# Attention of a transformer block: written orders for two steps' score and maxima tiles, by the kind of step

## The chip, the cores and the metric

The kernel is one transformer block in float32. It runs as one program on one core of a Trainium2 chip. The metric is the device time of the whole program in microseconds (us). Before the change it is 2805.59 us, the median of three runs (2802.46 to 2810.95). A profile was taken of one execution. The engines are named as the profile names them: PE (TensorE, with PEld for its weight loads), DVE (VectorE), ACT (ScalarE), POOL (GpSimd) and SP (the queue that issues most DMAs).

## What is computed

```python
def _A_ref(x, wqkv, wo):                       # S = 2048 rows, D = 576, H = 32 heads of Dh = 18
    qkv = (x @ wqkv).reshape(B, S, 3, H, Dh).transpose(2, 0, 3, 1, 4)
    q, k, v = qkv[0], qkv[1], qkv[2]
    scores = jnp.einsum("bhqd,bhkd->bhqk", q, k) * Dh ** -0.5
    p = _softmax(scores, axis=-1)
    o = jnp.einsum("bhqk,bhkd->bhqd", p, v)
    return o.transpose(0, 2, 1, 3).reshape(B, S, D) @ wo

mod = (_silu(c) @ w_mod).reshape(1, 6, 1, -1)  # sa, ca, ga, sb, cb, gb
h = _layernorm(x) * (1 + ca) + sa
x = x + ga * _A_ref(h, wqkv, wo)
h = _layernorm(x) * (1 + cb) + sb
x = x + gb * ((_sigmoid(h @ w_gate) * (h @ w_up)) @ w_down)
```

The change touches the scores, the softmax and their product with v, nothing else.

## The kernel before

The program has three parts: projections of q, k and v up to about 235 us, attention from there to about 1533 us, and the gated layer to the end. Attention runs as 32 units. A unit is two heads and half of the queries (1024), and it has 16 steps (`kt`), one for each 128 keys. A step makes four score tiles of 128 keys by 512 queries (two heads, two query halves). Each is one matmul into a PSUM bank (line 1055, called **t** here, t0 and t1 for the two heads), followed by an exponential on ACT from that bank into SBUF (line 1059). The products with v, called **values** (line 629), follow two steps later: four matmuls side by side into one bank that collects a whole unit.

The exponential needs each query's maximum first. The function `maxima` makes it ahead, for the unit after the current one, with eight more score tiles for each two steps, this time 128 queries by 512 keys (line 524, called **m**). Six of the eight are reduced on DVE (line 530). The other two belong together: ACT takes max(s, 0) of the first into a buffer `over` (line 533, called **r**), and DVE takes the second tile and `over` to one maximum (line 535, called **x**). At the end of a unit's maxima DVE reduces them once more (line 542, `nm`); in `spread`, `nm` is transposed (line 555), split on ACT and DVE (lines 559, 560) and written by DMA into rows of q.

All these tiles, t, m and the transposes, take their bank from `bank()`, a ring of seven: a tile is written into the bank of the tile seven before it, so its matmul waits until ACT or DVE has read that one. The two heads lie on different rows of the PE, so a t and an m of different heads that follow each other run at the same time; the kernel always puts tiles in such couples.

A unit's results are taken in the next unit: `taken` copies the values' bank on ACT (line 646); `outputs` transposes the copy with four matmuls into one bank of the ring (line 656), then DVE takes the reciprocals of the sums from that bank (line 661), ACT copies the same bank out (line 672), and POOL scales. While a bank is read by DVE for the reciprocals, the copy on ACT waits for it.

The order on PE, DVE and ACT is the order in which the code is written. Two steps, kt even and odd, go by one pair of strings. There are two pairs of strings. The "halved" one cuts the second step's values into two halves of 256 columns and is used when no row work of the other kind (projections of attention's output, in units 15 to 21 and 27 to 31) is in those two steps; the other one is for steps with such work. The letters: v values, a and b their halves, m the next maxima tile (from `MAXIMA_H` or `MAXIMA`), t the next score tile (from `SIDES_H` or `SIDES`), k `taken`, s and w the places where `outputs`, `spread` and row work begin, c the place where begun ones go on:

```python
order = ("vmmtmmtsactt", "wmcmbkttmtmt") if halved else ("vtmmttmvtm", "ktmwttmctmm")
MAXIMA_H = ((1, 0), (0, 0), (1, 1), (0, 2), (0, 3), (1, 2), (0, 1), (1, 3))   # head, chunk of keys
SIDES_H = ((1, 0), (1, 1), (0, 1), (0, 0))                                     # query half, head
```

With r and x written for the two tiles that belong together, the halved pair of steps is: V, m1 r0, t0 m1, m0 t1, (s) A (c) t1 t0, (w) m0 (c) m1, B (k), t0 t1, x0 t1, m1 t0. It is the same in every pair of steps; `taken` acts in kt 0, `outputs` in kt 3 (at w, between the couples t1 t0 and m0 m1), `spread` in kt 12 (at s).

Of the kernel before, what the change touches and what calls it, by code (L numbers as in the profile page):

```python
# [24 lines left out]
S = 2048  # L25
# [14 lines left out]
LEAD = 6  # L40
FROM0, FROM1 = 15 * 16, 27 * 16 + 8
# [6 lines left out]

MAXIMA = ((1, 0), (0, 0), (1, 1), (0, 2), (1, 2), (0, 3), (0, 1), (1, 3))
SINGLE = (0, 1)  # L50
MAXIMA_H = ((1, 0), (0, 0), (1, 1), (0, 2), (0, 3), (1, 2), (0, 1), (1, 3))
SIDES_H = ((1, 0), (1, 1), (0, 1), (0, 0))
SIDES = ((0, 0), (0, 1), (1, 0), (1, 1))
ORDERED = 7
SEVENS = NB - 2
TURNS = {1: 1, 6: 2, 2: 4, 7: 3, 5: 5, 4: 7, 3: 6}
ROWS_FROM = 1
SECOND = 7 * NB


@with_exitstack
def tile_block(ctx, tc, x_in, wqkv, wo, w_gate, w_up, w_down, c_in, w_mod, out):
# [24 lines left out]
    turns = {"s": 0, "to": 64 + 4 * LEAD, "bank": 0}  # L87
# [188 lines left out]
    ws = dram.tile([NB, len(ORDER), P, 10 * P], F32R, name="ws")  # L276
# [97 lines left out]
    with tc.tile_pool(name="ln", bufs=2) as ln:  # L374
# [31 lines left out]
        order = ExitStack()  # L406
# [93 lines left out]
    def maxima():  # L500


        n = HW // P
        last = None
        for u in range(UNITS):
            qs, ks = heads(u)
            mx = mxs[u % 2]
            if u not in SINGLE and u - 2 in SINGLE:
                nc.gpsimd.memset(mx[:, 0:n, 1], LOWEST)
            for i in range(8 * n):  # L510
                if last is not None and i == (9 if u == 1 else 8):
                    if u == 1:
                        for _ in spread(*last):
                            pass
                    else:
                        state["spread"] = last
                qt = i // 8
                pairs = u not in SINGLE
                h, kc = (MAXIMA_H if state.get("halved") else MAXIMA)[i % 8]
                rows = slice(64 * h, 64 * h + 3 * DH)  # L520
                paired = pairs and h == 0 and kc < 2
                at = NCH if paired and kc == 0 else kc
                sp = bank()
                nc.tensor.matmul(  # L524
                    sp, qs[rows, qt * P : (qt + 1) * P],
                    ks[rows, at * 512 : (at + 1) * 512], start=True, stop=True,
                )
                to = mx[:, h * n + qt, kc : kc + 1]
                if not paired:
                    nc.vector.tensor_reduce(to, sp, axis=AX.X, op=ALU.max)  # L530
                elif kc == 0:
                    over = small.tile([P, 512], F32, name="over", bufs=1)
                    nc.scalar.activation(over, sp, AF.Relu)  # L533
                else:
                    nc.vector.tensor_tensor_reduce(  # L535
                        out=over, in0=sp, in1=over, scale=1.0, scalar=LOWEST,
                        op0=ALU.add, op1=ALU.max, accum_out=mx[:, h * n + qt, 0:1],
                    )
                if i < 8 * n - 1:
                    yield  # L540
            nm = small.tile([P, 2, n], F32, name="nm")
            nc.vector.tensor_reduce(
                nm.rearrange("p h t -> p (h t)"), mx, axis=AX.X, op=ALU.max, negate=True
            )
            last = (qs, nm)
            yield
        for _ in range(8):
            yield
        state["spread"] = last
# [19 lines left out]
    todo = maxima()  # L569
    state = {}  # L570

    def turn():
        if turns["s"] < turns["to"]:
            turns["s"] += 1
            next(todo, None)

    def run():
# [428 lines left out]
    follow = []  # L1006
# [3 lines left out]
    for u in range(UNITS):  # L1010
        half, p = divmod(u, H // 2)
        qs, ks = heads(u)
        if 0 < u < UNITS - 2:
            load_heads(u + 2)
        if u == H // 2:
            Os.append(big.tile([P, 8, 640], F32, name="big"))
        for kt in range(NT):
            step = u * NT + kt
            turns["to"] = 64 + 4 * LEAD + 4 * (step + 1)
            kcols = slice(kt * P, (kt + 1) * P)  # L1020
            if kt % 2 == 0:
                heavy = state.get("next") == "g"
                hold = heavy and (kt == 2 or kt == 12 and u < UNITS - 1)
                state["halved"] = step >= 10 and (hold or not heavy)
            halved = state["halved"]
            sides = iter(SIDES_H if halved else SIDES)
            probs = [None] * 4
            order = ("vmmtmmtsactt", "wmcmbkttmtmt") if halved else ("vtmmttmvtm", "ktmwttmctmm")
            for does in order[kt % 2]:
                if does == "m":  # L1030
                    turn()
                elif does == "k":
                    taken()
                elif does in "ws":
                    if kt == 3:
                        follow.append(outputs())
                        next(follow[-1], None)
                    if "spread" in state and halved == (does == "s"):
                        follow.append(spread(*state.pop("spread")))
                        next(follow[-1])  # L1040
                    if step >= FROM0 and not hold and halved == (does == "s"):
                        state["next"] = next(rows0 if step < FROM1 else rows1, None)
                elif does == "c":
                    while follow:
                        next(follow.pop(0), None)
                elif does == "v":
                    if step >= LAG:
                        values()
                elif does in "ab":
                    values(slice(0, 256) if does == "a" else slice(256, 512))  # L1050
                else:
                    c, h = next(sides)
                    sT = bank()
                    rows = slice(64 * h, 64 * h + 3 * DH + 2)
                    nc.tensor.matmul(  # L1055
                        sT, ks[rows, kcols], qs[rows, c * 512 : (c + 1) * 512], start=True, stop=True
                    )
                    pr = probs[2 * c + h] = ppool.tile([P, 512], F32, name=f"p{2 * c + h}")
                    state["exp"] = nc.scalar.activation(pr, sT, AF.Exp, scale=SCALE)  # L1059
            pending.append((half, p, kt, probs))  # L1060
            if u in (1, 3):
                if kt == 0:
                    a = big.tile([P, 8, 640], F32, name="big")
                    a = a.rearrange("p a b -> p (a b)")[:, 0 : 8 * D].rearrange("p (t c) -> p t c", t=4)
                    b = slots.tile([P, 2560], F32, name="w0")[:, 0 : 2 * D]
                    mods = load_mod(a, b, 1 + u // 2)
                    row = slots.tile([P, 2560], F32, name="w1")[:, 0:544]
                    weighed = weigh(mods)
                elif kt >= 5:
                    next(weighed, None)  # L1070
            elif u in (2, 4) and kt in (2, 4):
                takes = [(ga_b, None), (mcol2[:, 1, :], 0.0)] if u == 2 else [(mcol2[:, 0, :], 1.0), (gb_b, None)]
                if kt == 2:
                    weighed = modulate(row, mods[:1], HALVES, takes)
                next(weighed, None)
            if 4 * NT + 8 <= step < FROM0 and step % 4 != 3:
                next(downs, None)
            if step == FROM0:
                for _ in downs:
                    pass  # L1080
            if step == FROM1 - 1:
                for _ in rows0:
                    pass
                bgs.close()
                rawst = ExitStack()
                raws = rawst.enter_context(tc.tile_pool(name="raws", bufs=1, side="right"))
            if u == 30 and kt == 7:
                first = [load_block(raws, b, k, paced) for b, k in ((0, 0), (0, 1), (1, 1))]
            if u >= 30 and kt == 2:
                load_x(u - 30, f"k{u - 30}")  # L1090
            if u == UNITS - 1 and kt == 3:
                nc.sync.dma_start(oend[:, :, 0 : D - DL - 2 * DH], Os[1][:, :, DL : D - 2 * DH])
            if u == UNITS - 1 and kt == 9:
                for _ in rows1:
                    pass
                load_x(2, "w0")
                load_x(3, "w1")
                both = big.tile([P, 2, 5, 512], F32R, name="big")
                for i in range(2):
                    X[5 + i] = both[:, i]  # L1100
                    load_x(5 + i)
# [687 lines left out]
```

## Time and profile before

| what | value |
|---|---|
| median of three runs | 2805.59 us |
| span of the profiled execution | 2801.3 us |
| PE busy | 2766.6 us (99%) |
| DVE busy | 2302.7 us (82%) |
| ACT busy | 1607.0 us (57%) |
| attention's share of the span (first to last exponential) | 234.9 to 1533.0 us |
| granted PE clock | full in all but the first slice |

The profiled execution's own time is not listed apart from its span. The span lies 4.3 us under the median of the runs; what lies around it (the start and the end of the program) is not touched here. Matmuls and activations overlap their successors, so the duration of one instruction is longer than the time it keeps its engine; how far one start lies behind the other is the better measure. A timeline merges instructions of one line that follow each other, and shows in brackets the idle time before them and what ended it.

### The profile page before, as it was taken

To read this page: it belongs to the slowest core of one execution; us is meant where nothing else is said; L and a number is where in the kernel's file an instruction comes from. 1 tells how busy PE (TensorE), PEld (TensorE's weight loads), DVE (VectorE), ACT (ScalarE), POOL (GpSimd) and SP (SyncE) were. 2 spreads that over 40 slices of the span, in tenths; PEclk is the share of its full clock that TensorE was granted. 3 is DMA by queue.
4 is the path that set the end of the run, shared out by engine and by line. 5 is a ranking of instruction groups with operands and counts; after the bars stand their busy time and mean duration, and the time that the engine had idled before them with its cause. 6 is when DMAs were issued, how large, how long until landed. Compare 5 with 4: busy or idle time off the path is not lost.

```text
span 2801.3 us, 50850 instructions
## 1 busy us (share of the span) xinstructions
PE 2766.6 (99%) x18637; PEld 1830.4 (65%) x18637; DVE 2302.7 (82%) x4370; ACT 1607.0 (57%) x3051; POOL 816.2 (29%) x1077
## 2 busy tenths in 40 slices
PE   7999999999999999999999999999999999999999
PEld 5975444444444444444444888888888888888888
DVE  7278999999998888999883788888898677777777
ACT  3216999999999778999888322333333222222221
POOL 3125208887843111663113222222221100000000
PEclk9999999999999999999999999999999999999999
DMA  5344215444442120232126766667767966666663
GB/s 173 123 155 147 72 59 173 168 173 157 170 135 80 36 59 24 98 106 71 43 68 219 266 220 228 232 217 266 279 249 274 355 201 196 203 196 200 199 197 120
DMA packets 170778, 462.60 MB, mean 165 GB/s; under 512 B 21212, under 2 KB 88032, under 8 KB 160416
## 3 DMA queue, kind: packets, MB, share of 16 engines
q1 hardware_dynamic: 150064, 360.72, 38.7%
q0 software_dynamic: 20464, 98.62, 10.0%
q8 instruction: 147, 2.41, 0.4%
q14 instruction: 103, 0.84, 0.1%
HBM read 281.92 MB, written 176.82 MB: 164 GB/s over the span
## 4 chain that ended last, share of the span: by engine, by line
PE 93%; DVE 4%; issue 1%; DMA 1%; ACT 1%; POOL 0%; SPq 0%; DVEq 0%; ACTq 0%; POOLq 0%
PE x L1196 28%; PE o L629 19%; PE s L1055 12%; PE s L524 10%; PE d L1346 8%; PE d L1278 6%; PE s L310 4%; PE s L776 2%; PE s L363 1%; DVE mx L530 1%; PE s L656 1%; ACT p L1059 1%; DMA wq_raw<-in_A_wqkv_dram 0%; DVE Oa L1350 0%; DVE w L1186 0%
## 5 line engine op out<-in xcount | busy, mean ns | idle before, releaser
L1059 ACT ACTIVATE p<-s 128x512 f32<-128x512 f32 x2048 | 1078.1, 621 | 98.8 <-PE s L1055 83.5
L530 DVE TENSOR_REDUCE mx<-s 128x1 f32<-128x512 f32 x1568 | 993.8, 683 | 108.0 <-PE s L524 93.3
L629 PE MATMUL o<-p,vaug 128*32 128x256 f32 (+1 forms) x5848 | 592.4, 477 | 3.1 <-ACT p L1059 2.5
L1055 PE MATMUL s<-q,k 56*128 56x512 f32 x1920 | 516.6, 449 | 0.0
L524 PE MATMUL s<-k,q 54*128 54x512 f32 x1920 | 501.3, 427 | 2.6 <-DVE t L746 1.7
L524 PEld LDWEIGHTS s<-k,q 54*128 54x128 f32 x1920 | 275.6, 185 | 231.6 <-DVE mx L535 161.0
L1055 PEld LDWEIGHTS s<-q,k 56*128 56x128 f32 x1920 | 246.9, 184 | 242.7 <-issue 112.8
L1196 PE MATMUL x<-k,w 128*128 128x512 f32 x1512 | 368.6, 391 | 0.0
L1196 PEld LDWEIGHTS x<-k,w 128*128 128x128 f32 x1512 | 276.9, 188 | 53.1 <-issue 1.7
L629 PEld LDWEIGHTS o<-p,vaug 128*32 128x32 f32 x5848 | 115.4, 108 | 209.7 <-issue 130.7
L1346 PE MATMUL d<-wd,hh 128*128 128x288 f32 x1248 | 249.9, 295 | 2.4 <-DVE Oa L1350 2.4
L1196 PE MATMUL x<-big,w 128*128 128x512 f32 x1008 | 244.9, 391 | 2.1 <-DVE u L1690 1.4
L1196 PE MATMUL x<-w,w 128*128 128x512 f32 x1008 | 245.1, 391 | 0.0
L1196 PEld LDWEIGHTS x<-big,w 128*128 128x128 f32 x1008 | 185.1, 188 | 38.5 <-DVE u L1690 2.3
L1196 PEld LDWEIGHTS x<-w,w 128*128 128x128 f32 x1008 | 184.4, 188 | 34.3
L1346 PEld LDWEIGHTS d<-wd,hh 128*128 128x128 f32 x1248 | 202.2, 188 | 6.2 <-DVE Oa L1350 3.1
L1346 PE MATMUL d<-wd,hl 128*128 128x288 f32 x624 | 184.3, 295 | 0.0
L1350 DVE TENSOR_TENSOR Oa<-Oa,d 128x288 f32<-128x288 f32 x312 | 136.4, 452 | 54.8 <-PE d L1346 50.8
L535 DVE CUSTOM_DVE_ANT_0 over<-s,over 128x512 f32<-128x512 f32 x240 | 164.4, 685 | 0.7 <-ACT p L1059 0.3
L533 ACT ACTIVATE over<-s 128x512 f32<-128x512 f32 x240 | 150.1, 626 | 7.4 <-PE s L524 7.3
L1205 ACT ACTIVATE sg<-x 128x512 f32<-128x512 f32 x36 | 21.6, 599 | 207.8 <-PE x L1196 207.8
L1177 ACT CAST w<-S 128x768 fp32r<-128x768 f32 x71 | 59.4, 836 | 137.5 <-POOL S L1150 135.6
(274 smaller groups left out, 3889.8 us busy)
## 6 DMA issues: line engine op xcount, KB each, us to landing
ws<-w SPq DMA_DIRECT2D x126, 640.0 KB
w<-ws SPq DMA_DIRECT2D x126, 640.0 KB
wd<-wds SPq DMA_DIRECT2D x19, 1152.0 KB
k<-kd SPq DMA_DIRECT2D x60, 360.0 KB
wds<-w POOLq DMA_DIRECT2D x18, 1152.0 KB, 5.6
wtd<-t POOLq DMA_DIRECT2D x32, 576.0 KB, 4.8
wt<-wtd SPq DMA_DIRECT2D x64, 288.0 KB
wd<-wds SPq DMA_DIRECT2D x52, 288.0 KB
```

Of the source, the lines that this page charges most:

```text
L310: nc.tensor.matmul(acc, w, hT[:, t, cols], start=n == 0, stop=n == len(ts_) - 1)
L524: nc.tensor.matmul(sp, qs[rows, qt * P : (qt + 1) * P], ks[rows, at * 512 : (at + 1) * 512], start=True, stop=True,)
L530: nc.vector.tensor_reduce(to, sp, axis=AX.X, op=ALU.max)
L533: nc.scalar.activation(over, sp, AF.Relu)
L535: nc.vector.tensor_tensor_reduce(out=over, in0=sp, in1=over, scale=1.0, scalar=LOWEST, op0=ALU.add, op1=ALU.max, accum_out=mx[:, h * n + q ...
L629: nc.tensor.matmul(acc[32 * j : 32 * j + 32, cols], vaug[:, kt, (2 * p + h) * VW : (2 * p + h) * VW + 32], probs[2 * c + h][:, cols], star ...
L1055: nc.tensor.matmul(sT, ks[rows, kcols], qs[rows, c * 512 : (c + 1) * 512], start=True, stop=True)
L1059: state["exp"] = nc.scalar.activation(pr, sT, AF.Exp, scale=SCALE)
L1196: nc.tensor.matmul(acc[v], w[:, v, a, :], X[s][:, b, :], start=first and n == 0, stop=n == 6, skip_group_check=not first,)
L1278: nc.tensor.matmul(acc, a[:, rows], w[:, k, :], start=n == 0, stop=n == 2)
L1346: nc.tensor.matmul(acc[:, :HALF], a[:, f, rows], w[:, f, cols], start=n == 0, stop=n == 5)
L1350: nc.vector.tensor_add(Oa[:, t, cols], Oa[:, t, cols], acc[:, :HALF])
```

## The change

Six strings replace the two pairs. A string holds two steps, and each tile is named in it with its head, so that the maxima tiles and the score tiles of a couple are chosen by hand: t0 and t1 a score tile of head 0 or 1 (query halves in turn), m0 and m1 a maxima tile, r0 and x0 the two that belong together, V, A, B the values, K `taken`, O `outputs`, S `spread` alone, G `spread` or row work, c the place where begun ones go on.

```diff
-MAXIMA_H = ((1, 0), (0, 0), (1, 1), (0, 2), (0, 3), (1, 2), (0, 1), (1, 3))
-SIDES_H = ((1, 0), (1, 1), (0, 1), (0, 0))
-SIDES = ((0, 0), (0, 1), (1, 0), (1, 1))
+STEPS = {
+    "full": "V t0m1 r0t1 t0m1 V t1m0 K t0m1 G t1t0 m0 c t1 x0m1",
+    "half": "V m1t0 t0t1 m0m1 G A c r0m1 t1t0 B m1t0 m0t1 t1x0",
+    0: "V r0m1 m1t0 t0t1 G A c m1m0 t1x0 B K t0t1 m0m1 t0t1",
+    2: "V m0t1 t0m1 t1m0 O A c r0m1 t0m1 t1x0 G B c t0m1 t1t0",
+    4: "V m1r0 t0m1 t1m0 G A c t0t1 m1t0 B t1x0 m0t1 t0m1",
+    12: "V m0t1 m1t0 t0m1 S A c t1t0 m1m0 G B c r0t1 m1x0 t1t0",
+}
...
-            turns["to"] = 64 + 4 * LEAD + 4 * (step + 1)
+            turns["to"] = 64 + 4 * LEAD + 8 * (step // 2 + 1)
...
-                state["halved"] = step >= 10 and (hold or not heavy)
-            halved = state["halved"]
-            sides = iter(SIDES_H if halved else SIDES)
+                halved = step >= 10 and (hold or not heavy)
+                order = two_steps(STEPS[kt if halved and kt in STEPS else "half" if halved else "full"])
             probs = [None] * 4
-            order = ("vmmtmmtsactt", "wmcmbkttmtmt") if halved else ("vtmmttmvtm", "ktmwttmctmm")
-            for does in order[kt % 2]:
+            for does, h, c in order[kt % 2]:
                 if does == "m":
-                    turn()
+                    turn(h, c)
...
-                elif does in "ws":
-                    if kt == 3:
-                        follow.append(outputs())
-                        next(follow[-1], None)
-                    if "spread" in state and halved == (does == "s"):
+                elif does == "O":
+                    follow.append(outputs())
+                    next(follow[-1], None)
+                elif does in "SG":
+                    if "spread" in state:
```

`two_steps` turns a string into two lists, one for each step; the fifth score tile opens the second. A tile's number among its unit's maxima stays its place in the count, so the last of the eight in a string is the one after which `nm` is taken. "full" writes out the order that steps with row work had before. No instruction is added or taken away on PE, DVE or ACT, but for waits that need an instruction of their own.

**PE, unit 12, steps 2 and 3, where the unit's results are transposed.** In these rows `s` with a number is one tile in the ring, `q` and `k` the operands (k first: a maxima tile), `o<-p,vaug` the values, `oT` the copied results. Before:

```order
L629 MATMUL o<-p_9757,vaug 32x256
L1055 MATMUL s_9808<-q_1025,k_2233 128x512
L1055 MATMUL s_9812<-q_1025,k_2233 128x512
L656 MATMUL s_9821<-ident,oT 128x128 x4
L524 MATMUL s_9826<-k_2236,q_1021 128x512
L524 MATMUL s_9834<-k_2236,q_1021 128x512
L629 MATMUL o<-p_9771,vaug 32x256
```

Now:

```order
L1078 MATMUL s_9797<-q_1025,k_2233 128x512
L549 MATMUL s_9801<-k_2236,q_1021 128x512
L682 MATMUL s_9804<-ident,oT 128x128 x4
L655 MATMUL o<-p_9753,vaug 32x256
L655 MATMUL o<-p_9767,vaug 32x256
L655 MATMUL o<-p_9757,vaug 32x256
L655 MATMUL o<-p_9771,vaug 32x256
L549 MATMUL s_9818<-k_2236,q_1021 128x512
L549 MATMUL s_9822<-k_2236,q_1021 128x512
```

The four transposes stood between two couples of score tiles behind the values' first half; they now stand ahead of it, behind three couples.

**ACT, the same two steps.** `p` is an exponential's output, `over` that of r, `oT<-s` the copy of the transposed results. Before:

```order
L533 ACTIVATE over_9788<-s3_9786 128x512
L1059 ACTIVATE p2_9792<-s4_9790 128x512
L1059 ACTIVATE p3_9802<-s0_9800 128x512
L1059 ACTIVATE p1_9810<-s1_9808 128x512
L1059 ACTIVATE p0_9814<-s2_9812 128x512
L672 COPY oT_9749<-s3_9821 128x512
L1059 ACTIVATE p2_9843<-s6_9841 128x512
```

Now:

```order
L1082 ACTIVATE p1_9788<-s3_9786 128x512
L1082 ACTIVATE p0_9792<-s4_9790 128x512
L1082 ACTIVATE p3_9799<-s6_9797 128x512
L698 COPY oT_9749<-s1_9804 128x512
L558 ACTIVATE over_9820<-s2_9818 128x512
L1082 ACTIVATE p2_9827<-s4_9825 128x512
L1082 ACTIVATE p1_9839<-s6_9837 128x512
```

Five activations of these two steps stood ahead of the copy, now three do, and r stands behind it.

**DVE, unit 12, where the maxima of the unit after it end** (steps 8 to 11; `mx_1040` is that unit's, `mx_1039` the next one's). Before:

```order
L530 TENSOR_REDUCE mx_1040<-s_10057 128x1
L535 ISA over,mx_1040<-s_10072,over 128x512
L535 ISA mx_1040 128x1
L530 TENSOR_REDUCE mx_1040<-s_10079 128x1
L542 TENSOR_REDUCE nm<-mx_1040 128x16
L530 TENSOR_REDUCE mx_1039<-s_10097 128x1
```

Now:

```order
L555 TENSOR_REDUCE mx_1040<-s_10065 128x1
L555 TENSOR_REDUCE mx_1040<-s_10072 128x1
L560 ISA over,mx_1040<-s_10083,over 128x512
L560 ISA mx_1040 128x1
L567 TENSOR_REDUCE nm<-mx_1040 128x16
L555 TENSOR_REDUCE mx_1039<-s_10097 128x1
```

x was the last but one of DVE's seven operations of two steps and is now the last, with `nm` right behind it.

## Rows read from the trace of the kernel before

**Rows 1.** Windows, unit 12: stretch, us, busy PE PEld DVE ACT POOL, clock, DMA, GB/s.

```profile
700.00:738.40 38.40, 38.40 (x329) 15.77 (x325) 35.42 (x68) 37.27 (x76) 28.34 (x46) 1.00 0.52 186
```

**Rows 2.** Timeline of PE, unit 12: start, us, engine, line, operation, output<-inputs, count.

```profile
702.64 1.07 PE L629 MATMUL o<-p,vaug 128*32 128x512 f32 x8
...
705.18 0.50 PE L1055 MATMUL s<-q,k 56*128 56x512 f32 x2
705.61 0.66 PE L656 MATMUL s<-ident,oT 128*128 128x128 f32 x4
706.20 0.49 PE L524 MATMUL s<-k,q 54*128 54x512 f32 x2
706.62 0.64 PE L629 MATMUL o<-p,vaug 128*32 128x256 f32 x8
...
708.09 1.07 PE L629 MATMUL o<-p,vaug 128*32 128x512 f32 x8
...
717.42 1.07 PE L629 MATMUL o<-p,vaug 128*32 128x512 f32 x8
718.41 0.72 PE L524 MATMUL s<-k,q 54*128 54x512 f32 x3
...
719.30 0.64 PE L629 MATMUL o<-p,vaug 128*32 128x256 f32 x8
719.88 0.51 PE L1055 MATMUL s<-q,k 56*128 56x512 f32 x2
...
720.64 0.64 PE L629 MATMUL o<-p,vaug 128*32 128x256 f32 x8
721.21 0.51 PE L1055 MATMUL s<-q,k 56*128 56x512 f32 x2
...
722.12 1.07 PE L629 MATMUL o<-p,vaug 128*32 128x512 f32 x8
...
726.81 1.07 PE L629 MATMUL o<-p,vaug 128*32 128x512 f32 x8
...
731.74 1.06 PE L629 MATMUL o<-p,vaug 128*32 128x512 f32 x8
...
736.36 1.07 PE L629 MATMUL o<-p,vaug 128*32 128x512 f32 x8
...
741.07 1.06 PE L629 MATMUL o<-p,vaug 128*32 128x512 f32 x8
```

**Rows 3.** Timeline of PE's weight loads, steps 8 and 9 of unit 12.

```profile
719.99 0.41 PEld L524 LDWEIGHTS s<-k,q 54*128 54x128 f32 x2
...
721.68 0.18 PEld L524 LDWEIGHTS s<-k,q 54*128 54x128 f32 x1 [0.17 <-ACT p L1059]
```

**Rows 4.** Timeline of ACT, steps 2, 3, 8 and 9 of unit 12.

```profile
707.02 0.59 ACT L672 COPY oT<-s 128x512 f32<-128x512 f32 x1
707.72 2.07 ACT L1059 ACTIVATE p<-s 128x512 f32<-128x512 f32 x4
...
717.12 2.07 ACT L1059 ACTIVATE p<-s 128x512 f32<-128x512 f32 x4 [0.18 <-PE s L1055]
...
719.52 2.11 ACT L1059 ACTIVATE p<-s 128x512 f32<-128x512 f32 x4
721.81 2.07 ACT L1059 ACTIVATE p<-s 128x512 f32<-128x512 f32 x4 [0.17 <-PE s L1055]
```

**Rows 5.** Timeline of DVE, steps 2 and 3, then 8 to 11, of unit 12.

```profile
706.37 0.26 DVE L661 RECIPROCAL rec<-s 128x16 f32<-128x16 f32 x1 [0.32 <-PE s L656]
...
718.94 3.08 DVE L530 TENSOR_REDUCE mx<-s 128x1 f32<-128x512 f32 x5 [0.35 <-PE s L524]
...
723.32 0.22 DVE L542 TENSOR_REDUCE nm<-mx 128x16 f32<-128x64 f32 x1
723.65 3.08 DVE L530 TENSOR_REDUCE mx<-s 128x1 f32<-128x512 f32 x5
```

**Rows 6.** The exponentials' line: counts and durations in ns (min/median/max).

```profile
L1059 ACTq EVENT_SEMAPHORE  x1171: 17/17/296, 234.4 to 1531.8; - x196
```

More of the change, by code (lines that the diff above doesn't have):

```diff
@@ L58, with two_steps @@
 SECOND = 7 * NB
+def two_steps(text):
+    steps, scores = ([], []), 0
+    keys = {"r0": [0], "x0": [1], "m0": [2, 3], "m1": [0, 1, 2, 3]}
+    for word in text.split():
+        for does in (word[:2], word[2:]):
+            if not does:
+                continue
+            if scores % 4 == 0:
+                sides = {"t0": [0, 1], "t1": [0, 1]}
+            to = steps[scores >= 4]
+            if does in sides:
+                to.append(("t", int(does[1]), sides[does].pop(0)))
+                scores += 1
+            elif does in keys:
+                to.append(("m", int(does[1]), keys[does].pop(0)))
+            else:
+                to.append((does, None, None))
+    return steps
 @with_exitstack
@@ L518, in maxima @@
                 pairs = u not in SINGLE
-                h, kc = (MAXIMA_H if state.get("halved") else MAXIMA)[i % 8]
+                h, kc = state.get("at") or MAXIMA[i % 8]
                 rows = slice(64 * h, 64 * h + 3 * DH)
@@ L570, in tile_block, with turn @@
     state = {}
-    def turn():
+    def turn(*at):
         if turns["s"] < turns["to"]:
             turns["s"] += 1
+            state["at"] = at
             next(todo, None)
@@ L1023, in tile_block @@
                 hold = heavy and (kt == 2 or kt == 12 and u < UNITS - 1)
-                state["halved"] = step >= 10 and (hold or not heavy)
-            halved = state["halved"]
-            sides = iter(SIDES_H if halved else SIDES)
+                halved = step >= 10 and (hold or not heavy)
+                order = two_steps(STEPS[kt if halved and kt in STEPS else "half" if halved else "full"])
             probs = [None] * 4
-            order = ("vmmtmmtsactt", "wmcmbkttmtmt") if halved else ("vtmmttmvtm", "ktmwttmctmm")
-            for does in order[kt % 2]:
+            for does, h, c in order[kt % 2]:
                 if does == "m":
-                    turn()
-                elif does == "k":
+                    turn(h, c)
+                elif does == "K":
                     taken()
-                elif does in "ws":
-                    if kt == 3:
-                        follow.append(outputs())
-                        next(follow[-1], None)
-                    if "spread" in state and halved == (does == "s"):
+                elif does == "O":
[3 more added lines that the diff above has]
+                    if "spread" in state:
                         follow.append(spread(*state.pop("spread")))
                         next(follow[-1])
-                    if step >= FROM0 and not hold and halved == (does == "s"):
+                    if does == "G" and step >= FROM0 and not hold:
                         state["next"] = next(rows0 if step < FROM1 else rows1, None)
@@ L1045, in tile_block @@
                         next(follow.pop(0), None)
-                elif does == "v":
+                elif does == "V":
                     if step >= LAG:
                         values()
-                elif does in "ab":
-                    values(slice(0, 256) if does == "a" else slice(256, 512))
+                elif does in "AB":
+                    values(slice(0, 256) if does == "A" else slice(256, 512))
                 else:
-                    c, h = next(sides)
                     sT = bank()
```

## The prediction

> **What bounds the kernel now.** I read the windows first, then one unit of attention, instruction by instruction, on PE, then on ACT and DVE, to see who lets PE go. The change touches attention alone, some 1300 us of the 2801.3 us span. In a unit's 16 steps PE is busy without a break and ACT and DVE nearly so: 38.40, 37.27 and 35.42 of 38.40 us, at the full granted clock [rows 1]. A busy PE is not PE at its peak, so the question is what a pair of steps (one string of the order) costs and what of that is waiting.
>
> PE's own price of a pair is read from steps 8 and 9 [rows 2]. The whole values and the way to the next couple take 0.99 us (717.42 to 718.41). Three couples take 0.89 (to 719.30) or 0.91 (721.21 to 722.12). A half of the values takes 0.58 or 0.57. A couple alone takes 0.43 (705.18 to 705.61) or 0.42 (706.20 to 706.62), so each further couple adds 0.24 and two couples should take 0.66. Steps 8 and 9 show 0.76 for them (719.88 to 720.64). So PE alone would need 0.99 + 0.89 + 0.58 + 0.66 + 0.57 + 0.91 = 4.60 us; the trace has 4.70 and 4.69 (717.42 to 722.12 to 726.81).
>
> The missing 0.10 is a bank. The second of two weight loads that span 0.41 us begins at 719.99 + 0.41 - 0.18 = 720.22 [rows 3]; the tile goes into the bank that the exponential begun at 719.52 was reading [rows 4]. ACT is late there because it ran dry earlier: it idles 0.17 or 0.18 us once a pair [rows 4]. When it has work, its starts lie 0.48 us apart (five from 717.12 to 719.52) and nine operations end 4.51 us after the first start (721.63), which is 0.60 and then 0.49 each [rows 4]. From an exponential's end to the weight load that it frees are 0.05 us (721.63 to 721.68) [rows 3, 4]. DVE does one reduction each 0.60 us (five in 3.08, the last lasting 0.68) and idles 0.35 us once a pair [rows 5].
>
> Four pairs differ from the regular 4.69: steps 2, 3 take 5.45 (702.64 to 708.09), steps 12, 13 4.93, steps 14, 15 4.62 and steps 0, 1 4.71 [rows 2]. So a unit's eight pairs take 38.43 us (702.64 to 741.07), eight times 4.60 with the transposes' own 0.59 would be 37.4, and the difference is the most that an order can win.
>
> **The change part by part.** The order for steps with row work is written out again as it was, so the 37 pairs that use it stay. The other 219 change. No instruction goes away, and the groups between the values keep their sizes: three couples, two and three. So PE's 4.60 stays, and the sum is one of waits.
>
> Transposes of a unit's results (31 times). Before, they split two couples: 705.18 to 706.62 is 1.44 us where 0.66 would do, 0.78 for the transposes. Now they stand where PE changes from couples to values anyway and cost their own 0.59 (705.61 to 706.20) [rows 2]. That is 0.19 us won for each unit, if nothing waits.
>
> The copy behind the reciprocals (the same 31 times) takes it back. The copy on ACT waits for DVE's reciprocals, and these stand on DVE behind all three reductions of the pair's first three couples, as they did before; but the transposes are ready earlier, and on ACT r and all exponentials but three now stand behind the copy. From the start of the pair: the first couple begins at 0.99, its reduction 0.53 later (718.41 to 718.94), three reductions and the reciprocals end at 1.52 + 1.80 + 0.26 = 3.58 [rows 2, 5]. The trace doesn't show the copy's own delay after that: the smallest row is the 0.05 above, the largest the 0.39 from 706.63 to 707.02, where ACT was busy with an exponential [rows 4, 5]. I take 0.10, since the small row is a bare release. So the copy begins at 3.68; ACT was free for it at 1.59 + 3 x 0.48 = 3.03. Behind it r ends at 3.68 + 0.60 + 0.49 = 4.77, its bank is free at 4.82. Seven tiles on, that bank is asked for in the couple behind B, which PE reaches at 0.99 + 0.89 + 0.59 + 0.58 + 0.91 + 0.57 = 4.53: 0.29 us of waiting. The last couple needs the bank of the exponential behind r, free at 5.31, and 0.42 after such a load the next values begin (720.22 to 720.64): the pair takes 5.73 where it took 5.45. 31 x 0.28 = **+8.7 us**; with 0.05 and 0.39 instead of 0.10 it would be +7.1 and +17.7, without any wait (4.60 + 0.59 = 5.19) -8.1.
>
> On this the Trainium skill ("PSUM — Partial Sum Buffer", section on bank collisions) says that two engines may not access one PSUM bank and quadrant at the same time, ACT and DVE reads included. It is why the copy cannot simply start at 3.03; if it could, this term would be the -8.1. No row here shows the two apart.
>
> `nm` behind x. Before, `nm` (0.33 us from 723.32 to 723.65) fell into DVE's idle 0.35 [rows 5]. Now x is the pair's last tile and `nm` follows it. Counted from the couple behind B, DVE's last three begin at 0.53, 1.13 and 1.73; x, taken as long as a reduction, ends at 2.41, `nm`, which reads its result, begins 0.05 later, and DVE is free at 2.46 + 0.33 = 2.79. The next pair's first couple comes 0.91 + 0.99 = 1.90 after, so its reduction begins 0.89 instead of 0.53 behind it and frees its bank at 0.89 + 0.68 + 0.05 = 1.62. The tile beside r wants that bank at 0.89 + 0.58 = 1.47: 0.15 us. The fourth reduction is late by as much, and I add 0.10 for the tile that follows it in its bank. The pair takes 4.60 + 0.25 and the 0.04 of the next term, 4.89 instead of 4.69, in the 22 units where both pairs have the new order: **+4.4 us** (ends: 0, if DVE makes it up, and +6.6).
>
> The regular pairs. ACT's nine operations now begin with the first couple. The ninth ends 4.51 after the first start, 0.53 or 0.60 behind that couple (707.72 behind 706.62 + 0.57; 721.81 behind 721.21) [rows 2, 4], and frees its bank at 5.09 or 5.16. The third couple of the next pair must load for that bank 0.42 before its group ends, at 4.60 + 0.89 - 0.42 = 5.07. So 0.02 to 0.09 is missing instead of 0.10, partly shared by two pairs. The smaller delay, 0.53, is that of exponentials whose one wait needs no instruction of its own; 1171 such instructions stand before the 2048 exponentials now [rows 6], and in the changed program the units 8 to 12 have 150 on ACT instead of 275. I take 0.04 for three pairs of 25 units: **-3 us** (ends 0 and -7.5).
>
> Steps 0, 1: the two maxima tiles of the first couples are reduced one after the other, the second ends at 0.53 + 0.60 + 0.68 = 1.81 behind the first couple and can be loaded over at 1.86; x wants the bank at 0.89 + 0.58 + 0.24 = 1.71. With 0.05 for the third couple the pair takes 4.60 + 0.15 + 0.05 = 4.80 instead of 4.71, 27 times **+2.4 us** (0 to +4). Steps 12, 13: `spread` stays in its place, and I take 0.05 of their 0.24 over a regular pair, 30 times **-1.5 us** (0 to -3.6). Steps 4, 5 and 14, 15 have hardly a wait to lose; 0. SP and POOL issue the same DMAs at the same steps; the copy's POOL users have a unit's time.
>
> The sum is 8.7 + 4.4 - 3 + 2.4 - 1.5 = +11.0 us. The profiled 2801.3 us would become 2812.3; the median of the runs lies 4.3 above that span, so **2816.6 us**, 0.39% more. A measurement of this kernel can tell about 0.3% (8.4 us) from no change.
>
> **The rivals.** (1) Faster: ACT and DVE drain in time everywhere. It decides at the copy: if it begins before about 3.35 in its pair, r's bank is free at 4.5 and nothing waits. Then steps 2, 3 give -8.1, and the regular and other pairs come from their 4.69 towards 4.60, some 110 pairs by 0.09, -10: 2787; with half of it 2796. For it speaks that the new strings spread r, x and the maxima so that ACT gets a score tile in nearly each couple. Against it speak the three reductions ahead of the reciprocals, which no order on PE overtakes. (2) No change: the ring still has seven banks, ACT still has nine operations of 0.49 in 4.60 us, and a wait taken from one couple comes back at another; the copy's wait and the won 0.19 cancel: 2805.6, with 2799 to 2813 around it. The Trainium skill ("Perfetto Trace Analysis", Optimization Strategy) has a rule for this: the same gap again and again can mean too little PSUM for the next tile; by it an order in the same ring gives the time of before. ACT's 0.17 to 0.18 in each pair agrees with it. (3) Worse than forecast: the copy begins 0.39 behind the reciprocals, and the exponentials it delays reach into steps 4, 5: 2826 or somewhat more.
>
> **How the numbers follow.** Chances: 0.50 for the forecast with rival 3 (slower by over 0.3%), 0.32 for rival 2 (within 0.3%), 0.18 for rival 1 (faster by over 0.3%). The forecast's own range, from the terms' ends, is 2809 to 2828. To hold 8 in 10 the range takes in rival 2 and the upper half of rival 1: 2794 to 2829.
>
> **What would show it.** Right: in steps 2, 3 the pair takes about 5.7 us, ACT idles some 0.6 us ahead of the copy, and a weight load behind B waits for ACT's r; the pair after `nm` takes 4.9 with a weight load waiting for DVE. Wrong: steps 2, 3 under 5.3 us, or the copy right behind the third exponential; regular pairs at 4.60, or at more than 4.75, would say that my reading of the ring is off.

## The result, and the profile after

The changed kernel takes 2814.14 us (median of 8 runs, 2812.34 to 2818.12); the kernel before took 2806.23 us in the runs beside it (8 runs). The ratio is 1.0026, with an interval of 1.0016 to 1.0036: slower by about 8 us. The forecast was 2816.6, 11 us above its base; the direction, the place and the size of the largest term held. The term for `nm` didn't, and the wins counted for the regular pairs and for steps 12, 13 mostly stayed out.

The two traces are compared pair by pair, from the start of one whole values to the next. The table has the medians over the halved pairs of all units, in us, good to 0.01, for before, after and the eight experiments told below.

| kernel | steps 0, 1 | 2, 3 | 4, 5 | 6, 7 | 8, 9 | 10, 11 | 12, 13 | 14, 15 | sum |
|---|---|---|---|---|---|---|---|---|---|
| before | 4.71 | 5.46 | 4.64 | 4.68 | 4.68 | 4.69 | 4.93 | 4.63 | 38.42 |
| predicted | 4.80 | 5.73 | 4.64 | 4.64 | 4.64 | 4.89 | 4.88 | 4.63 | 38.85 |
| after | 4.83 | 5.72 | 4.63 | 4.65 | 4.66 | 4.67 | 4.93 | 4.60 | 38.69 |
| e1 steps 2, 3 as before | 4.83 | 5.38 | 4.64 | 4.66 | 4.66 | 4.66 | 4.93 | 4.60 | 38.36 |
| e2 copy first | 4.84 | 5.23 | 4.63 | 4.66 | 4.66 | 4.67 | 4.93 | 4.60 | 38.22 |
| e3 steps 0, 1 as "half" | 5.20 | 5.72 | 4.61 | 4.66 | 4.66 | 4.67 | 4.93 | 4.60 | 39.05 |
| e4 "half" alone new | 4.74 | 5.45 | 4.64 | 4.68 | 4.67 | 4.66 | 4.93 | 4.63 | 38.40 |
| e5 copy first, steps 0, 1 as before | 4.74 | 5.34 | 4.63 | 4.65 | 4.66 | 4.66 | 4.93 | 4.60 | 38.21 |
| e6 transposes a couple earlier | 4.84 | 5.87 | 4.63 | 4.66 | 4.66 | 4.67 | 4.93 | 4.60 | 38.86 |
| e7 before, copy first | 4.72 | 5.46 | 4.71 | 4.66 | 4.68 | 4.69 | 4.93 | 4.63 | 38.48 |
| e8 `nm` twice | 4.83 | 5.72 | 4.63 | 4.66 | 4.66 | 4.79 | 4.93 | 4.60 | 38.82 |

Steps 2 and 3 carry the loss, 0.26 us in the median over 31 units. Here they are in unit 12 of the changed kernel. PE first, the start of the pair, the transposes, the couple behind B and the next pair (start, us, engine, line, operation, count):

```profile
705.40 1.06 PE L655 MATMUL o<-p,vaug 128*32 128x512 f32 x8
...
707.30 0.66 PE L682 MATMUL s<-ident,oT 128*128 128x128 f32 x4
...
709.92 0.49 PE L1078 MATMUL s<-q,k 56*128 56x512 f32 x1
710.21 0.50 PE L549 MATMUL s<-k,q 54*128 54x512 f32 x1
...
711.12 1.07 PE L655 MATMUL o<-p,vaug 128*32 128x512 f32 x8
```

The timelines of DVE and of ACT in the same steps; the bracket tells the idle time and what ended it:

```profile
706.93 1.89 DVE L555 TENSOR_REDUCE mx<-s 128x1 f32<-128x512 f32 x3 [0.21 <-PE s L1078]
708.73 0.25 DVE L687 RECIPROCAL rec<-s 128x16 f32<-128x16 f32 x1
```

```profile
705.15 3.54 ACT L1082 ACTIVATE p<-s 128x512 f32<-128x512 f32 x7
709.07 0.59 ACT L698 COPY oT<-s 128x512 f32<-128x512 f32 x1 [0.38 <-DVE rec L687]
709.55 0.60 ACT L558 ACTIVATE over<-s 128x512 f32<-128x512 f32 x1
```

The reader should follow one chain. On DVE stand three reductions, then the reciprocals (to 708.98). ACT stands idle until 709.07, copies, then does r, which ends at 710.15. The couple behind B is written from 709.92, but its second matmul starts only at 710.21, where in a couple without a wait both start together (both at 728.85 in the same place of steps 10, 11): PE waits 0.29 us for r's bank, just where the prediction had put it. The pair takes 5.72 us (705.40 to 711.12), where [rows 2] show 5.45.

That the wait is in nearly every unit is seen in the view of the copy's line, after and (second fence) before: what its engine sat idle for, in us, and how often. The reciprocals held up ACT in 30 of 31 copies now, in 2 before.

```profile
L698 ACT COPY oT<-s x31: 585/585/673, 280.6 to 1512.3; 128x512 f32<-128x512 f32 x31
its engine sat idle before it (us, times) until:
  DVE rec L687: 13.8, 30
```

```profile
L672 ACT COPY oT<-s x31: 586/736/747, 281.6 to 1503.7; 128x512 f32<-128x512 f32 x31
its engine sat idle before it (us, times) until:
  DVE rec L661: 0.7, 2
```

`nm` is the place that went otherwise. DVE around it in unit 12 after, and the row of PE's weight loads behind it:

```profile
725.92 0.68 DVE L560 CUSTOM_DVE_ANT_0 over<-s,over 128x512 f32<-128x512 f32 x1
726.52 0.08 DVE L560 DVE_READ_ACCUMULATOR2_ANT mx<- 128x1 f32 x1
726.64 0.22 DVE L567 TENSOR_REDUCE nm<-mx 128x16 f32<-128x64 f32 x1
726.78 3.89 DVE L555 TENSOR_REDUCE mx<-s 128x1 f32<-128x512 f32 x6
```

```profile
729.30 0.18 PEld L1078 LDWEIGHTS s<-q,k 56*128 56x128 f32 x1 [0.16 <-DVE mx L555]
```

`nm` stands last and DVE goes straight on, but the next reduction begins 0.14 us after `nm` began (726.64 to 726.78), not 0.33 as in [rows 5]. In [rows 5] PE had not yet written the next tile. Before the change PE began that tile only at 723.12:

```profile
723.12 0.72 PE L524 MATMUL s<-k,q 54*128 54x512 f32 x3
```

The reduction follows 0.53 later (723.65), the distance that the prediction itself gives from a couple to its reduction. So part of the 0.33 was waiting, not `nm`. One load later in the pair still waits for DVE (the bracket of 729.30), but the pair takes 4.66 here, like the two pairs before it in the table.

### The profile page after: what moved, and what is told of

Read it like the earlier page. It is cut to its first block, busy times and chain, and to the rows that moved or that the text cites. A ratio compares the mean times of both kernels' runs of the same rounds, so it can differ in the third digit from the quotient of the medians.

```text
span 2810.8 us, 50381 instructions
## 1 busy us (share of the span) xinstructions
PE 2777.8 (99%) x18637; PEld 1857.8 (66%) x18637; DVE 2307.0 (82%) x4370; ACT 1613.0 (57%) x3051; POOL 815.0 (29%) x1077
## 4 chain that ended last, share of the span: by engine, by line
PE 90%; DVE 5%; issue 2%; DMA 1%; POOL 1%; ACT 1%; SPq 0%; DVEq 0%; ACTq 0%; POOLq 0%
PE x L1219 26%; PE o L655 18%; PE s L549 12%; PE s L1078 11%; PE d L1369 8%; PE d L1301 6%; PE s L335 4%; PE s L802 2%; PE s L388 1%; DVE mx L555 1%; DMA out_dram<-Oa 1%; PE s L682 1%; DVE w L1209 0%; DVE st L208 0%; DVE Oa L1373 0%
## 5 line engine op out<-in xcount | busy, mean ns | idle before, releaser
L1082 ACT ACTIVATE p<-s 128x512 f32<-128x512 f32 x2048 | 1062.9, 618 | 77.1 <-PE s L1078 57.0
L549 PE MATMUL s<-k,q 54*128 54x512 f32 x1920 | 557.3, 442 | 1.2 <-DVE t L772 1.1
L1078 PE MATMUL s<-q,k 56*128 56x512 f32 x1920 | 544.5, 434 | 1.5 <-DVE mx L555 1.4
L549 PEld LDWEIGHTS s<-k,q 54*128 54x128 f32 x1920 | 262.8, 184 | 312.0 <-DVE mx L555 128.0
L1078 PEld LDWEIGHTS s<-q,k 56*128 56x128 f32 x1920 | 265.6, 185 | 165.6 <-DVE mx L555 55.7
```

The lines of the kernel that those rows point to most:

```text
L549: nc.tensor.matmul(sp, qs[rows, qt * P : (qt + 1) * P], ks[rows, at * 512 : (at + 1) * 512], start=True, stop=True,)
L1078: nc.tensor.matmul(sT, ks[rows, kcols], qs[rows, c * 512 : (c + 1) * 512], start=True, stop=True)
```

## The experiments

**e1: steps 2 and 3 in the order of before.** All else is the changed kernel.

```diff
-    2: "V m0t1 t0m1 t1m0 O A c r0m1 t0m1 t1x0 G B c t0m1 t1t0",
+    2: "V m1r0 t0m1 m0t1 G A c t1t0 O m0 c m1 B t0t1 x0t1 m1t0",
```

> The changed kernel with one string altered: steps 2 and 3 get the order of before again, with the transposes between two couples behind A; all other strings stay new. Theory (the copy on ACT waits for the reciprocals behind three reductions, which costs 0.28 us in steps 2, 3 of each unit): steps 2, 3 of unit 12 fall from 5.72 to 5.4 to 5.5 us, the kernel to about 2806 us, ratio to the kernel before 1.000 (0.999 to 1.001). Rival A (the loss is spread over the new strings, steps 2, 3 only show it): it stays within 2 us of 2814, ratio 1.0025.

Measured: 2805.17 us, ratio 1.0000 (0.9991 to 1.0008) to the kernel before; steps 2, 3 take 5.38. The whole net loss lies in this one string: steps 0, 1 still take 0.12 more than before, and what steps 2, 3 and the regular pairs win makes it up. In unit 12 the copy again stands behind a run of exponentials without idle time:

```profile
707.45 2.12 ACT L1082 ACTIVATE p<-s 128x512 f32<-128x512 f32 x4
709.36 0.69 ACT L698 COPY oT<-s 128x512 f32<-128x512 f32 x1
```

The 5.38 is 0.08 less than the same string takes before, though only its neighbours changed; e5 comes back to that.

**e2: the copy ahead of the reciprocals**, which then read the copy in SBUF, not the bank (not in the last unit). The new strings stay.

```diff
...
+            nc.scalar.copy(oT, tp.rearrange("p b q -> p (b q)"))
+            tq = oT.rearrange("p (b j e) -> p j b e", j=4, e=32)
         nc.vector.reciprocal(rec, tq[:, :, :, DH])
...
-        nc.scalar.copy(oT, tp.rearrange("p b q -> p (b q)"))
-        tq = oT.rearrange("p (b j e) -> p j b e", j=4, e=32)
```

> The changed kernel with all its strings, but the copy on ACT no longer waits for the reciprocals: it reads the transposed bank first, and DVE takes the reciprocals from the copy in SBUF (not in the last unit). Theory (the wait of the copy is the cause): the copy begins about 3.0 to 3.1 us into steps 2, 3 instead of 3.66, no weight load behind B waits for r, the pair takes 5.2 to 5.3 us instead of 5.72; 31 units by 0.45 are 14 us, so 2799 to 2801 us, ratio to the kernel before 0.998. Rival B (the transposes' new place ahead of A is what costs, by delaying the values and the tiles behind): the pair stays at 5.6 or more and the kernel at 2812 to 2814. Rival C (DVE, which now waits for the copy, takes the place of ACT): the pair falls by less than 0.2 us, with weight loads that wait for DVE, and the kernel to 2808 or more.

Measured: 2800.71 us, ratio 0.9985 (0.9977 to 0.9994): faster than both kernels, 13 us under the changed one. Steps 2, 3 take 5.23, near the 5.19 that the prediction gives PE alone. ACT and DVE in unit 12 (the pair begins at 701.84):

```profile
701.57 3.54 ACT L1085 ACTIVATE p<-s 128x512 f32<-128x512 f32 x7
704.92 0.67 ACT L690 COPY oT<-s 128x512 f32<-128x512 f32 x1
705.43 0.66 ACT L558 ACTIVATE over<-s 128x512 f32<-128x512 f32 x1
```

```profile
705.70 0.25 DVE L692 RECIPROCAL rec<-oT 128x16 f32<-128x16 f32 x1 [0.44 <-ACT oT L690]
```

The copy begins 3.08 us into the pair instead of 3.67 and ACT has no idle time. The wait now stands on DVE (0.44), where PE hardly feels it. The edit also frees the transposes' own bank earlier, but the tile that takes this bank next was not late in the changed kernel: it is the matmul of 709.92, 4.52 us into the pair, where the prediction has 4.53 without a wait. So the dependency of the copy on the reciprocals is the cause, not the place of the transposes and not a lack of banks.

**e3: steps 0 and 1 by the string of the regular steps**, with `taken` put behind B.

```diff
-    0: "V r0m1 m1t0 t0t1 G A c m1m0 t1x0 B K t0t1 m0m1 t0t1",
+    0: "V m1t0 t0t1 m0m1 G A c r0m1 t1t0 B K m1t0 m0t1 t1x0",
```

> The changed kernel with one string altered: steps 0 and 1 get the regular string with the copy of the values' bank behind B; all others stay new. Theory (two maxima tiles in the first two couples make x's bank late, which costs 0.12 us a unit): steps 0, 1 of a unit fall from 4.83 to about 4.70, and 27 times 0.12 are 3 us: 2811 us, ratio to the kernel before 1.0015. Rival (ACT's extra copy costs it in any order): no change against 2814.

Measured: 2820.66 us, ratio 1.0056 (1.0044 to 1.0068); steps 0, 1 take 5.20. Both expectations missed it. PE's row at the start of steps 2 in unit 12 tells why, with ACT's copy of the values' bank:

```profile
710.10 1.07 PE L655 MATMUL o<-p,vaug 128*32 128x512 f32 x8 [0.47 <-ACT oT L672]
```

```profile
708.45 1.12 ACT L1082 ACTIVATE p<-s 128x512 f32<-128x512 f32 x2
709.41 0.64 ACT L672 COPY oT<-o 128x512 f32<-128x512 f32 x1
```

All values of a unit go into one bank. The next unit's first values wait until `taken` has copied it, and in this string three activations (r and two exponentials) of the couples ahead of B stand before that copy on ACT; in the string for steps 0, 1 only one does. The view of the values' line has this wait in all units: PE and its weight loads sat idle until that copy for 33.5 us, 55 times, and for 7.1 us, 27 times, in the changed kernel. 5.20 less the 0.47 is 4.73. So the changed kernel's string has its reason, which no term of the prediction saw, and which the experiment found by breaking it.

**e4: the new regular string alone**; steps 0, 1, 2, 3, 4, 5, 12 and 13 keep the order of before.

```diff
-    0: "V r0m1 m1t0 t0t1 G A c m1m0 t1x0 B K t0t1 m0m1 t0t1",
+    0: "V m1r0 t0m1 m0t1 G A c t1t0 m0 c m1 B K t0t1 x0t1 m1t0",
...
-    12: "V m0t1 m1t0 t0m1 S A c t1t0 m1m0 G B c r0t1 m1x0 t1t0",
+    12: "V m1r0 t0m1 m0t1 G A c t1t0 m0 c m1 B t0t1 x0t1 m1t0",
```

> Only the regular string is new; steps 0, 2, 4 and 12 get the order of before. Theory (the regular string wins about 0.03 us a pair, fewer waits of ACT that need an instruction of their own): regular pairs at 4.66 instead of 4.69, some 90 pairs, 2803 to 2804 us, ratio to the kernel before 0.999. Rival (the new regular string costs in the pairs that follow another string): 2808 us or more.

Measured: 2805.8 us, ratio 1.0004 (0.9996 to 1.0013): no difference that can be told. Steps 8, 9 gain 0.01 and steps 10, 11 gain 0.03, with `nm` behind x here too. Steps 6, 7 gain nothing (4.68), nor do 14, 15 (4.63), which follow pairs in the old order. That suggests that the gain of a regular pair needs a new one ahead of it; no run tests this by itself. The theory is right in sign, and the gain is smaller than expected. The rival (2808 us or more) falls.

**e5: e2 with steps 0 and 1 in the order of before.** (String as in e4.)

> The copy-first kernel with, besides, the order of before in steps 0 and 1. Theory: steps 0, 1 cost 0.09 to 0.12 us more in the new order (4.83 against 4.71 before and 4.74 in the run that had four old orders), because x wants a bank that DVE has not read yet; in the old order they come back to 4.71 to 4.74, steps 2, 3 stay at 5.23, and 27 x 0.10 = 2.7 us come off the 2800.7 of the copy-first kernel: about 2798. Rival: the wait at x's bank only moves the work of DVE that is in arrears to steps 2 and 3, whose new order was made to follow the new one; then steps 0, 1 fall to 4.74 and steps 2, 3 rise to about 5.33: 2801.

Measured: 2801.76 us, ratio 0.9989 (0.9980 to 0.9998). The rival was right: steps 0, 1 fall to 4.74, steps 2, 3 rise to 5.34, and the two together are 10.08, against 10.07 in e2. PE's weight loads for the third couple and the transposes of steps 2, 3 in unit 12, in e5 (the pair begins at 701.15) and, in the second fence, in e2 (701.84):

```profile
702.63 0.18 PEld L1081 LDWEIGHTS s<-q,k 56*128 56x128 f32 x1 [0.19 <-ACT p L1085]
702.64 0.18 PEld L549 LDWEIGHTS s<-k,q 54*128 54x128 f32 x1
703.13 0.42 PEld L682 LDWEIGHTS s<-ident,oT 128*128 128x128 f32 x4 [0.30 <-ACT p L1085]
```

```profile
703.22 0.18 PEld L1081 LDWEIGHTS s<-q,k 56*128 56x128 f32 x1
703.22 0.18 PEld L549 LDWEIGHTS s<-k,q 54*128 54x128 f32 x1
703.74 0.42 PEld L682 LDWEIGHTS s<-ident,oT 128*128 128x128 f32 x4 [0.34 <-ACT p L1085]
```

In e5 the third couple's loads wait for an exponential and come 1.48 us into the pair, in e2 1.38. The bracket at the transposes stands in both and is no extra wait. ACT is late by as much: its copy of the values' bank begins 0.64 us before the pair in e5 (700.51) and 0.75 in e2 (701.09). The old order ends steps 0, 1 sooner, but with ACT in arrears by a tenth of a microsecond, and the next pair pays. The same can be the 0.08 by which e1's steps 2, 3 are under before; that wasn't tested apart.

**e6: the transposes one couple earlier**, so that the reciprocals stand behind two reductions.

```diff
-    2: "V m0t1 t0m1 t1m0 O A c r0m1 t0m1 t1x0 G B c t0m1 t1t0",
+    2: "V m0t1 t0m1 O c t1m0 A r0m1 t0m1 t1x0 G B c t0m1 t1t0",
```

> The transposes one couple earlier, so that the reciprocals stand behind two reductions; the copy still waits for them. Theory (the copy begins when the reciprocals are done, and these stand behind the reductions issued before them): the reciprocals end at 1.52 + 1.20 + 0.26 = 2.98 into the pair instead of 3.58, the copy begins at about 3.07 instead of 3.66, r's bank is free at 4.2 and nothing behind B waits for ACT; splitting the couples costs 0.18 as it did before the change, so steps 2, 3 take 4.60 + 0.59 + 0.18 = 5.37 to 5.42 instead of 5.72, and the kernel about 2814.1 - 31 x 0.32 = 2804. Rival (the place of the transposes doesn't matter, ACT is late from its own work): steps 2, 3 stay at 5.6 to 5.8 or rise by the 0.18, 2814 to 2819.

Measured: 2820.72 us, ratio 1.0055 (1.0043 to 1.0068); steps 2, 3 take 5.87. The first half of the expectation (the copy's start) holds to the hundredth, the second (the pair's time) fails. The rival's time is the nearer one: it allowed a rise by 0.18, and 0.15 came. Its reason, that the place doesn't matter because ACT is late from its own work, holds only in part, since the copy does begin earlier. ACT and the weight loads in unit 12 (the pair begins at 707.36):

```profile
710.44 0.59 ACT L698 COPY oT<-s 128x512 f32<-128x512 f32 x1 [0.28 <-DVE rec L687]
710.92 0.60 ACT L1082 ACTIVATE p<-s 128x512 f32<-128x512 f32 x1
711.41 0.60 ACT L558 ACTIVATE over<-s 128x512 f32<-128x512 f32 x1
```

```profile
711.07 0.18 PEld L1078 LDWEIGHTS s<-q,k 56*128 56x128 f32 x1 [0.16 <-ACT oT L698]
711.57 0.18 PEld L549 LDWEIGHTS s<-k,q 54*128 54x128 f32 x1 [0.32 <-ACT p L1082]
```

The copy begins at 3.08 of the pair, as worked out (3.07). But it still waits 0.28 for the reciprocals, and now the exponential of the third couple stands behind it (710.92), which the expectation had left out. x is seven tiles after that one and waits for its bank, the load of 711.57, 0.05 behind the exponential's end. Here an earlier start of the copy was worth nothing, because another tile moved behind the copy.

**e7: the kernel before, with the copy ahead of the reciprocals** (the edit of e2).

> The kernel before, with the copy ahead of the reciprocals, which read the copy. Theory: in the order of before the copy lost little by its wait, since five activations stood ahead of it; steps 2, 3 go from 5.46 to the 5.38 that PE needs by itself there (4.60 + 0.78), 31 x 0.08 = 2.5 us at most: 2803 to 2805. Rival: the copy's wait for DVE costs as much in the order of before as in the new one (0.49 us a unit), then 31 x 0.4 us: about 2793.

Measured: 2808.06 us, ratio 1.0012 (1.0003 to 1.0021). The rival falls: without the new order the edit wins nothing, as the two idle times in 31 copies before would have it. The expected small gain didn't come either: steps 2, 3 stay at 5.46 and steps 4, 5 rise by 0.07. On DVE the reciprocals move behind the copy, with 0.29 us of idle time:

```profile
710.83 0.26 DVE L666 RECIPROCAL rec<-oT 128x16 f32<-128x16 f32 x1 [0.29 <-ACT oT L663]
```

**e8: the changed kernel with the reduction to `nm` written twice.** The text has the two one behind the other; on DVE one reduction came to stand between them.

```diff
             nc.vector.tensor_reduce(
                 nm.rearrange("p h t -> p (h t)"), mx, axis=AX.X, op=ALU.max, negate=True
             )
+            nc.vector.tensor_reduce(
+                nm.rearrange("p h t -> p (h t)"), mx, axis=AX.X, op=ALU.max, negate=True
+            )
```

> The changed kernel with the reduction to nm written twice, one behind the other: 0.136 us more on DVE in 32 places. Theory now (nm's place behind x costs next to nothing, since nm keeps DVE 0.14 and not 0.33 us and DVE makes it up in the same pair): the pair after nm stays at 4.67 to 4.70, the kernel at 2814 to 2815. Rival (the prediction's: what DVE is late by is handed on to PE at x's bank and again at the tile that follows it there): 0.14 to 0.28 more, 4.81 to 4.95, 22 to 25 times, 2817 to 2820.

Measured: 2815.94 us, ratio 1.0041 (1.0029 to 1.0054); the pair after `nm` takes 4.79 instead of 4.67. The rival, that lateness of DVE is handed on to PE, is the nearer one: it said 0.14 to 0.28 more for the pair, and 0.12 came, 2 us on the kernel where it had 3 to 6. DVE and one weight load in unit 12:

```profile
732.62 0.22 DVE L567 TENSOR_REDUCE nm<-mx 128x16 f32<-128x64 f32 x1
732.75 0.68 DVE L555 TENSOR_REDUCE mx<-s 128x1 f32<-128x512 f32 x1
733.35 0.21 DVE L570 TENSOR_REDUCE nm<-mx 128x16 f32<-128x64 f32 x1
733.48 3.15 DVE L555 TENSOR_REDUCE mx<-s 128x1 f32<-128x512 f32 x5
```

```profile
735.41 0.18 PEld L1081 LDWEIGHTS s<-q,k 56*128 56x128 f32 x1 [0.30 <-DVE mx L555]
```

Each `nm` keeps DVE 0.13 to 0.14 us. The first fits into what DVE has to spare; the second, 0.13, comes out at PE as 0.12 (the idle time until DVE grows from 0.16 in the row of 729.30 to 0.30).

## Why the prediction was right, and where not

- **Copy behind the reciprocals, +8.7: right, in size and in mechanism.** Predicted 5.73, measured 5.72; 31 x 0.26 = 8.1 us. The copy begins at 3.67 (predicted 3.68), the wait at r's bank is 0.29 (0.29). e1 shows that this string is the loss, e2 that the dependency is the cause. ACT's idle time ahead of the copy is 0.38 in unit 12 and 13.8 / 30 = 0.46 in the mean, less than the 0.6 forecast. The row of 705.15 shows why: ACT was in a run of seven exponentials without idle time and was through the third of this pair only at 708.69, 3.29 into the pair, where the prediction has it free at 3.03.
- **Transposes' new place, 0.19 won: right, and hidden by the wait.** With the copy first, it shows: 5.23 in e2 against 5.38 in e1, 0.15 of the 0.19, behind the same steps 0, 1. The two differ in the copy's place too, but in e1 the copy has next to no idle time to lose, and in the order of before e7 won nothing by it.
- **`nm`, +4.4: wrong, the mis-sized term.** The failed step is "DVE is free at 2.46 + 0.33". The 0.33 is the distance from `nm` to the next start in [rows 5], and part of that was PE's tile not being there; start to start it is 0.14 when the tile is there. With 0.14 the prediction's own working gives a bank free at 1.43 where 1.47 is wanted: no wait, and the pair took 4.67 instead of 4.89. Of the chain behind it e8 shows one half: its second `nm` delays the reductions after the first, and 0.13 on DVE come out as 0.12 at the tile that follows the one beside r in its bank (735.41), where the prediction had put 0.10. The other half, a wait at the tile beside r itself, stays out in unit 12 of e8 too: that tile's row starts 1.54 behind the pair's first couple (732.04 to 733.58), as in the changed kernel (726.07 to 727.61).
- **Regular pairs, -3: right in sign.** 0.02 to 0.03 instead of 0.04 for each in the median; summed over steps 6 to 11 the traces differ by 1.3 us outside units 16 to 20 and by 0.7 with them. The instructions that only wait fell on the exponentials' line from 1171 [rows 6] to 766:

```profile
L1082 ACTq EVENT_SEMAPHORE  x766: 17/17/296, 233.8 to 1539.7; - x192
```

- **Steps 0, 1, +2.4: right by its number (0.12 for 0.09), wrong as a term of its own.** e5 shows that what this pair gives back the next one takes. Measured together, steps 0 to 3 went from 10.17 to 10.55, +0.38 where the two terms sum to 0.37.
- **Steps 12, 13, -1.5: wrong, nothing was won** (4.93 both; summed +0.5, most of it in units 18 to 20). Steps 14, 15 won 0.03, which was put at 0.
- **Not in the sum: units 16 to 20**, where row work lies between. Their time rose by 3.2 us in the two traces (231.8 to 235.0), of which steps 2, 3 explain 1.5 (0.37 in each of units 18 to 20, and 0.27 and 0.14). About 1.2 us lie in other pairs of units 16 to 19 (steps 8, 9 of unit 16 from 4.89 to 5.16, steps 12, 13 of unit 18 from 5.36 to 5.53) and are there in e1 too, so they belong to the other strings; the remaining 0.5 us lie in unit 20, 0.43 of them in steps 12, 13, and in its last four steps e1, with the same strings, has 0.9 more than after. For steps 12, 13 of unit 20 the traces show a wait of another kind, DVE for POOL, before (first fence) and after:

```profile
1075.47 0.17 DVE L200 TENSOR_TENSOR sd<-r 128x8 f32<-128x8 f32 x1 [1.26 <-POOL r L197]
```

```profile
1082.02 0.17 DVE L225 TENSOR_TENSOR sd<-r 128x8 f32<-128x8 f32 x1 [1.86 <-POOL r L222]
1082.11 1.88 DVE L555 TENSOR_REDUCE mx<-s 128x1 f32<-128x512 f32 x3
```

Reductions stand behind this row work on DVE, and PE's idle time until a reduction is 1.41 us there, against 0.93 before. No experiment was made on these units; what lengthens the other pairs stays open.

- **What is luck.** Summed over all halved pairs the traces differ by 9.1 us where the prediction has 11.0: 7.6 in steps 2, 3 (forecast 8.7), 2.7 in steps 0, 1 (2.4), 0.5 in steps 12, 13 (-1.5), -0.7 in steps 6 to 11 (-3 and +4.4 for `nm`) and -1.0 in steps 4, 5, 14 and 15 (0). The 4.4 us too many for `nm` and the 4.3 us of wins that did not come nearly cancel. That the total lies within 2.5 us of the forecast is luck in that part; that steps 2, 3 took 5.72 is not.
- **The rivals.** "Faster" named its condition rightly: the copy would have to begin before about 3.35. It began at 3.67; in e2 it begins at 3.08, and the predicted 5.19 comes as 5.23. "No change" rested on the rule for gaps that come again and again (the Trainium skill, "Perfetto Trace Analysis", Optimization Strategy). The Trainium skill says this there of the engine that should be saturated, which is PE here; the 0.17 to 0.18 that the prediction set beside it are ACT's. With the same seven banks e1 and e2 take 0.34 and 0.49 us off one pair, so in steps 2, 3 it was not space that was short. On the Trainium skill's words about two engines at one bank ("PSUM — Partial Sum Buffer", section on bank collisions): the copy's idle time ends with DVE's reciprocals (709.07), as a wait of the program would have it, so no run here shows what the bank itself would do.
- **The chances.** The measured 0.26% lies just under the prediction's own border of 0.3% between "no change" and "slower", its interval on both sides of it. But the mechanism of "no change", waits that cancel, is not what the traces show. The forecast's 0.39% was too high by the `nm` term; without it the sum would have been +6.6, too low, since the wins it counts on did not come.

The better version is e2: 2800.71 us. e5 lies 1 us above it, within what these runs can tell.

## What to carry to other kernels

When two engines read one result and the reader on which a ring of buffers hangs stands idle until the other is done, put that reader first and let the other read its copy: here that turned an order 8 us slower than before into one 4 us faster. In the order of before, where that reader had hardly any idle time, the same edit won nothing (e7). Price an operation by the distance to the next start only where the row shows that nothing else was awaited; a gap in the row may be the producer's. Neighbouring stretches can hand their arrears on, as in e5, so measure an order over both.

## What had not been expected of the hardware

The reciprocals take as long from SBUF as from the bank (0.25 us in e2 and after, 0.26 before), so reading the copy does not lengthen the instruction, though DVE stands idle for 0.44 us ahead of it in e2. And a third fewer waiting instructions on ACT's exponentials (766 for 1171) brought regular pairs only 0.02 to 0.03 us: ACT's starts already lay 0.48 us apart in its runs before.
